# State products behind the preceding pair's outputs, and two of seven products in halves, in a scan kernel fused with a PReLU layer

## The chip, the cores and the metric

The kernel runs on one core of one Trainium2 chip. The metric is the device time of one execution in microseconds (us). The kernel before takes 374.15 us, the median of three runs (373.92 to 374.18). The profile is of one further execution of 374.39 us; its span, from the first instruction to the last, is 372.4 us.

## The reference

Two blocks follow one another. The first is a state-space scan over 4 batches, 8 heads and 768 tokens, in chunks; the second is a layer of width 2048 with a PReLU, on 3072 tokens of 256 numbers each. All is float32.

```python
# scan, per chunk (x: 4x8x768x32, a: 4x8x768, B and C: 4x8x768x16)
cum = np.cumsum(la, axis=-1)                       # la = log a of the chunk
L = np.exp(cum[..., :, None] - cum[..., None, :]) * causal
M = np.einsum('bhin,bhjn->bhij', Cc, Bc) * L       # gram products of C and B, decayed
y_intra = np.einsum('bhij,bhjd->bhid', M, xc)
y_inter = np.einsum('bhin,bhnd->bhid', Cc, state) * np.exp(cum)[..., None]
state = decay_full * state + sum_j(decay_from_j * B_j x_j)     # the state products
# layer (x: 3072x256, the scan's output with heads side by side)
h = x @ w_in                                       # 256 -> 2048
g = np.maximum(h, 0) + alpha * np.minimum(h, 0)
out = g @ w_out                                    # 2048 -> 256
```

(`state = ...` is cut to its meaning.) The kernel uses chunks of 128 tokens. Two chunks make a pair, and there are twelve pairs, 0 to 11; two pairs (512 tokens) make one of six groups.

## The kernel before

The first group goes through the layer with plain matrix products. Each later group goes through it as a two-by-two block product with seven products instead of eight, on each side. The 2048 hidden columns are taken in four quads (z = 0 to 3) per group; so there are 20 quads. A quad has seven products of the first part, from tokens to hidden values, which collect in two PSUM tiles A and Y. While they run, the seven products of the second part, from hidden values to outputs, run for the quad before. One product is two matrix instructions of 128x256 and appears as four records in the trace.

The order of a quad is fixed here. `after(j)` is a place at which other work is put in between:

```python
        first(A, lambda q: wi[:, q, 0, 0], b11, True)
        m1 = tile_of(wtp, "m1", "wt")
        nc.scalar.copy(out=m1, in_=A)
        after(1)
        first(Y, lambda q: s1[:, q], t1, True)
        m5 = tile_of(wtp, "m5", "wt")
        nc.scalar.copy(out=m5, in_=Y)
        after(2)
        after(3)
        first(A, lambda q: s2[:, q], t2)
        u2 = tile_of(wtp, "u2", "wg")
        nc.scalar.copy(out=u2, in_=A)
        after(4)
        nc.vector.tensor_tensor(out=Y, in0=Y, in1=u2, op=ALU.add)
        after(5)
        first(A, lambda q: wi[:, q, 1, 0], t3)
        c22 = tile_of(wtp, "c22", "wg")
        nc.vector.tensor_tensor(out=c22, in0=A, in1=m5, op=ALU.add)
        after(6)
        first(Y, lambda q: s4[:, q], b22)
        g12, g22, g21, g11 = (tile_of(gp, "gt", "gt") for i in range(4))
        prelu(g12, Y, z, 0)
        prelu(g22, c22, z, 1, (nc.scalar,))
        nc.scalar.copy(out=Y, in_=m1)
        prelu(g22, c22, z, 1, (nc.vector,))
        after(7)
        after(8)
        ta, tb, tc_, td = (tile_of(gp, "gt", "gt") for i in range(4))
        nc.gpsimd.tensor_tensor(out=tc_, in0=g22, in1=g12, op=ALU.subtract)
        first(A, lambda q: wi[:, q, 1, 1], t4)
        prelu(g21, A, z, 1)
        after(9)
        after(10)
        first(Y, lambda q: wi[:, q, 0, 1], b21)
        prelu(g11, Y, z, 0)
        for o, x0, x1 in ((ta, g12, g11), (tb, g22, ta), (td, tb, g21)):
            eng = nc.vector if g == NG - 1 and z == NZ - 1 and o is not td else nc.gpsimd
            eng.tensor_tensor(out=o, in0=x0, in1=x1, op=ALU.subtract)
        blocks[g, z] = {1: g11, 2: g21, 3: g22, 4: td, 5: ta, 6: tb, 7: tc_}
        after(11)
        after(12)
        after(13)
        after(14)
```

The products of the second part:

```python
    def product(g, z, n):

        if z == 0 and n == 1:
            ms[g] = [t.rearrange("p (h t) -> p h t", h=2)
                     for t in [bank(i) for i in range(3)] + m5_bank]
        i, h = (LAST if g == NG - 1 else HALVES)[n]
        s1, s2, s4 = out_sums
        for p in range(2):
            q = 2 * z + p
            w = {1: wq[:, q, 0, 0], 2: wq[:, q, 1, 0], 3: s4[:, q], 4: wq[:, q, 1, 1],
                 5: s1[:, q], 6: s2[:, q], 7: wq[:, q, 0, 1]}[n]
            nc.tensor.matmul(ms[g][i][:, h], w, blocks[g, z][n][:, p],
                             start=(q == 0 and h == 0), stop=(q == NQ - 1),
                             skip_group_check=True)
```

The scan of a pair of the next group is a generator of nine stages, put one by one into the places of the quads. Stage by stage for the pairs 4 to 11 (`fine`): transposes of B and C; four pieces of the decay matrix by scans on VectorE; state products and states; gram products of C and B and their multiplication by the decays in two stages; outputs and their copies. The state products are here, with `states`, which updates the state on VectorE and masks it on GpSimd:

```python
        def added(dps):
            dps = dps.rearrange("p (k m) -> p k m", m=P)
            for k in range(nk):
                for w in range(KC):
                    ws = slice(64 * w, 64 * w + 64)
                    nc.tensor.matmul(dps[ws, k], bn[:, k, ws], xt[:, k, w * P : (w + 1) * P],
                                     start=True, stop=True, tile_position=(0, 64 * w),
                                     skip_group_check=True)
            return dps
        # ... cut: states(dps)
        if fine:
            for k in range(2):
                for w in range(2):
                    half_decays(k, w)
                    if k == 1 and w == 1:
                        spread_c()
                    yield
        # ... cut: other pairs, gram products
            if fine:
                states(added(ss_tile()))
                c_decayed()
            yield
            gram = products_bc()
        # ... cut: multiplication of the gram products with the decays
        yield
        y = [ss_tile()[:, : 2 * Q].rearrange("p (k t) -> p k t", k=2) for w in range(KC)]
        # ... cut
        for k in range(2):
            if st[k] is not None:
                for w in range(KC):
                    ws = slice(64 * w, 64 * w + 64)
                    nc.tensor.matmul(y[w][:, k], st[k][ws], cd[ws, k], start=not begun, stop=False,
                                     tile_position=(64 * w, 0), skip_group_check=True)
                begun = True
        # ... cut: the outputs of the chunk itself, 32x128 products in columns of 32
        for w in range(KC):
            nc.scalar.copy(out=xts[g][:, w, q * Q : (q + 2) * Q],
                           in_=y[w].rearrange("p k t -> p (k t)"))
```

Two of the four gram tiles are in the small PSUM pool, the other two take the place of A and Y. Which stage falls into which place, and where the products of the second part go, say these tables (z, j) and j. A quad with gram products (z even, while scans are left) uses `with_gram`, the others `without`:

```python
    steps = {(0, 1): 0, (0, 2): 0, (0, 5): 0, (0, 9): 0, (0, 13): 0, (1, 1): 0, (1, 5): 0,
             (1, 12): 1, (1, 14): 1, (2, 1): 1, (2, 2): 1, (2, 5): 1, (2, 9): 1, (2, 13): 1,
             (3, 1): 1, (3, 5): 1, (3, 12): 2, (3, 14): 2}
# ... cut
    with_gram = {3: 1, 5: 2, 7: 3, 8: 5, 11: 7, 13: 6, 14: 4}
    without = {3: 1, 5: 2, 7: 3, 8: 5, 9: 7, 13: 6, 14: 4}
# ... cut, in after(j):
            places = with_gram if nxt < NP and z % 2 == 0 else without
            if i and j in places:
                product(*divmod(NZ + i - 1, NZ), places[j])
# ... cut
            if nxt + steps.get((z, j), NP) < NP:
                ssm(nxt + steps[z, j])
```

Of the kernel before, what the change touches and what calls it, by code (L numbers as in the profile page):

```python
# [9 lines left out]
F32 = mybir.dt.float32  # L10
U32 = mybir.dt.uint32
U16 = mybir.dt.uint16
ALU = mybir.AluOpType
# [9 lines left out]
def kernel(  # L23
# [25 lines left out]
    nc = tc.nc  # L49
# [276 lines left out]
    held = {}  # L326
    bns = {}

    def identity_bank():
# [82 lines left out]
    def spare():  # L412

        return ps_h.tile([P, GT], F32, name="hp", tag="hp")

    def pair(gp):

        b, c = divmod(2 * gp, CPB)
        nat, abc, xt, ap = loads["p", gp]
        last = c + 2 == CPB  # L420
        dec = work.tile([P, 2, H, Q], F32, name="dec")
        dv = dec.rearrange("p k h t -> p k (h t)")

# [37 lines left out]
            yield  # L461


        tp = spare() if gp == 1 else ss_tile()
        if gp == 0:
            keep_warm(tp, 3, Q)
# [23 lines left out]
        fine = gp >= 2 * GC // 2  # L490
        if gp < 2:
            spread_c()
        if gp == 0:
# [2 lines left out]
            dps = spare()  # L496
            keep_warm(dps, 6, Q)
            yield
        bn = bns.pop(gp) if gp in bns else pair_loads(gp)
        if gp == 1:  # L500
            c_decayed()
            dps = spare()
# [1 line left out]
        elif gp:  # L504
            yield

        nk = 1 if last else 2  # L510
        st = [masked.get(b)]
        new = work.tile([P, 2, P], F32, name="state")
        sm = work.tile([P, 2, P], F32, name="sm")

        def added(dps):
            dps = dps.rearrange("p (k m) -> p k m", m=P)
            for k in range(nk):
                for w in range(KC):
                    ws = slice(64 * w, 64 * w + 64)
                    nc.tensor.matmul(dps[ws, k], bn[:, k, ws], xt[:, k, w * P : (w + 1) * P],  # L520
                                     start=True, stop=True, tile_position=(0, 64 * w),
                                     skip_group_check=True)
            return dps

        def states(dps):
            for k in range(nk):
                old = state.get(b)
                if old is None:
                    nc.scalar.copy(out=new[:, k], in_=dps[:, k])
                else:  # L530
                    e = (k + 1) * Q - 1
                    nc.vector.scalar_tensor_tensor(out=new[:, k], in0=old, scalar=pf[:, e : e + 1],
                                                   in1=dps[:, k], op0=ALU.mult, op1=ALU.add)
                state[b] = new[:, k]
            nc.gpsimd.tensor_tensor(out=sm[:, :nk], in0=new[:, :nk],
                                    in1=hmask.unsqueeze(1).to_broadcast([P, nk, P]), op=ALU.mult)
            st.extend(sm[:, k] for k in range(nk))
            masked[b] = st[-1]

        if fine:  # L540
            for k in range(2):
                for w in range(2):
                    half_decays(k, w)
                    if k == 1 and w == 1:
                        spread_c()
                    yield
        else:
            if gp > 1:
                states(added(ss_tile()))
                c_decayed()  # L550
# [33 lines left out]
        if gp == 0:  # L584
            gram = products_bc()
            dps = added(dps)
            yield
            c_decayed()
            times(dec[:, :, :2], one_less(gram))
        elif gp == 1:  # L590
            gram = products_bc()
            g0 = one_less(gram)
            yield
            decays(1)
            states(dps)
            times(dec[:, :, :2], g0)
        else:
            if fine:
                states(added(ss_tile()))
                c_decayed()  # L600
            yield
            gram = products_bc()
        for i, r in enumerate(r for r in ((2, 3, 0, 1) if fine else (3, 2, 1, 0) if gp > 1 else range(4))
                              if r in gram):
# [6 lines left out]
        yield  # L611


        y = [ss_tile()[:, : 2 * Q].rearrange("p (k t) -> p k t", k=2) for w in range(KC)]
        if gp < 2:
            keep_warm(y[0].rearrange("p k t -> p (k t)"), 2 - gp)
        begun = False
# [7 lines left out]
        for k in range(2):  # L625
            for w in range(KC):
                for q in range(4):
                    h = 4 * w + q
                    nc.tensor.matmul(y[w][32 * q : 32 * q + 32, k], xt[:, k, h * D : (h + 1) * D],  # L629
                                     dec[:, k, h], start=False, stop=True,  # L630
                                     tile_position=(0, 32 * q), skip_group_check=True)
        g, q = divmod(2 * gp, GC)
        if q == 0:
            xts[g] = xtp.tile([P, KC, GT], F32, name="xT")
# [98 lines left out]
    LAST = {**HALVES, 4: (3, 1)}  # L733
    blocks = {}

    def product(g, z, n):

        if z == 0 and n == 1:
            ms[g] = [t.rearrange("p (h t) -> p h t", h=2)
                     for t in [bank(i) for i in range(3)] + m5_bank]  # L740
        i, h = (LAST if g == NG - 1 else HALVES)[n]
        s1, s2, s4 = out_sums
        for p in range(2):
            q = 2 * z + p
            w = {1: wq[:, q, 0, 0], 2: wq[:, q, 1, 0], 3: s4[:, q], 4: wq[:, q, 1, 1],
                 5: s1[:, q], 6: s2[:, q], 7: wq[:, q, 0, 1]}[n]
# [231 lines left out]
    for f in range(FIRST, NF):  # L978
        if f in (5, 10):
            load_pair(3 + f // 10)  # L980
        if f == 5:
            load_rows(1)
        hidden(0, f)
        if f <= 10:
            ssm(2)
        if f >= 9:
            ssm(3)
        for i in {FIRST: (5,), FIRST + 1: (6, 7)}.get(f, ()):
            convert_a(*pieces[i])
        convert_next(first=f > FIRST)  # L990
        if f == 8:
            bns[3] = pair_loads(3)
        if f == 8:
            rows_clamp(1)
            held["pr"] = rows_scan(1)
            rows_out(1)
        output(f - FIRST)
        if f in in_steps:
            weight_sums(wi, in_sums, 0, in_steps[f])
    early[0] = None  # L1000
    token_sums(1)
    ssm(2 * GC // 2, 2)


    steps = {(0, 1): 0, (0, 2): 0, (0, 5): 0, (0, 9): 0, (0, 13): 0, (1, 1): 0, (1, 5): 0,
             (1, 12): 1, (1, 14): 1, (2, 1): 1, (2, 2): 1, (2, 5): 1, (2, 9): 1, (2, 13): 1,
             (3, 1): 1, (3, 5): 1, (3, 12): 2, (3, 14): 2}

    late_sums = {(0, 2): ((wqt, out_sums, 0, 0),), (0, 4): ((wqt, out_sums, 0, 1),),
# [6 lines left out]
    last_out = {3: ((0, 0),), 5: ((1, 0),), 7: ((2, 0),), 8: ((3, 0),), 11: ((0, 1),), 13: ((1, 1),),  # L1016
            14: ((2, 1), (3, 1))}

    with_gram = {3: 1, 5: 2, 7: 3, 8: 5, 11: 7, 13: 6, 14: 4}
    without = {3: 1, 5: 2, 7: 3, 8: 5, 9: 7, 13: 6, 14: 4}  # L1020
    for i in range(NZ * (NG - 1)):
        g, z = divmod(NZ + i, NZ)
        nxt = 2 * g + 2

        def after(j, g=g, z=z, i=i, nxt=nxt):
            places = with_gram if nxt < NP and z % 2 == 0 else without
            if i and j in places:
                product(*divmod(NZ + i - 1, NZ), places[j])
            if i == 0:
                for f, half in last_out.get(j, ()):  # L1030
                    output(NF - LATE + f, half)
            if (i, j) in ((0, 13), (1, 2)):
                store_first(i)
            for args in late_sums.get((i, j), ()):
                weight_sums(*args)
            if g > 1 and z == 0 and j in (5, 9, 13, 14):
                if j == 5:
                    comb[0] = combine(g - 1)
                next(comb[0], None)
            if g > 1 and z in (1, 3) and j == 11:  # L1040
                finish(g - 1, z // 2)
            if nxt + steps.get((z, j), NP) < NP:
                ssm(nxt + steps[z, j])
            if nxt < NP and (z, j) == (3, 7):
                token_sums(g + 1)
            ahead = nxt + {(1, 3): 1, (3, 8): 2}.get((z, j), NP)
            if ahead < NP:
                if ahead == 6:
                    rows_turn(1, held["pr"])
                bns[ahead] = pair_loads(ahead)  # L1050

# [37 lines left out]
```

## Time and profile before

| engine | busy us | share of the span | instructions |
|---|---|---|---|
| TensorE, products | 365.4 | 98% | 2223 |
| TensorE, weight loads | 295.1 | 79% | 2223 |
| VectorE | 243.1 | 65% | 462 |
| GpSimd | 201.1 | 54% | 211 |
| ScalarE | 179.7 | 48% | 384 |

The products of the first part (line 772 of the kernel before, into `hp`, which is A and Y) are 33.7% of the chain that ended last, those of the second part (line 747, into `bank`) 32.4%. State products are line 520, transposes 469, gram products 570, outputs 622 and 629, the prelu 755 on ScalarE and 757 on VectorE, the copy that refills Y with m1 line 801. A line of the timeline begins with the start and the length in us. In brackets stands how long the engine was idle and what ended it. Products overlap in the engine's pipeline, so the lengths are not their cost; the distance from start to start is.

### The profile page before, as it was taken

The page shows a single profiled execution, that of the slowest core. Times are in us where ns is not written, and L with a number is a line of the kernel's source. Part 1 is how long each engine was busy: PE and PEld are TensorE (multiplying, and loading weights), DVE is VectorE, ACT ScalarE, POOL GpSimd, SP SyncE. Part 2 cuts the span into 40 slices and gives each one's busy share as a digit, 9 for nine tenths or more (in the row PEclk, how much of TensorE's full clock was granted, in tenths as well). Part 3 has the DMA queues.
Part 4 walks back from the last instruction along what each step waited for, and adds up shares of the span by engine and source line. Part 5 has one row for each costly group of instructions (what it writes and reads, how often), then busy time and mean ns, then how long its engine had stood idle before and what let it go on. Part 6 is the DMA issues. An engine that isn't in the chain of part 4 may idle for free.

```text
span 372.4 us, 6183 instructions
## 1 busy us (share of the span) xinstructions
PE 365.4 (98%) x2223; PEld 295.1 (79%) x2223; DVE 243.1 (65%) x462; ACT 179.7 (48%) x384; POOL 201.1 (54%) x211
## 2 busy tenths in 40 slices
PE   8989999999999999999999999999999999999996
PEld 8766666578788888788788788788788788888884
DVE  7897979976448548738638847637848644643364
ACT  1647866435355355444444445445535525553541
POOL 4775565778929754724644525555445355264512
PEclk9999999999999999999999999999999999999999
DMA  7889999911176301005603703702801001001004
GB/s 147 181 151 322 276 284 202 181 31 58 48 136 112 72 3 56 2 0 79 134 3 61 151 2 54 159 0 45 167 2 29 2 0 23 8 0 30 1 0 85
DMA packets 121878, 30.71 MB, mean 82 GB/s; under 512 B 93736, under 2 KB 117752, under 8 KB 121848
## 3 DMA queue, kind: packets, MB, share of 16 engines
q1 hardware_dynamic: 116736, 29.74, 36.0%
q10 hardware_dynamic: 5112, 0.59, 1.1%
q8 instruction: 17, 0.28, 0.3%
q14 instruction: 13, 0.11, 0.1%
HBM read 26.98 MB, written 3.34 MB: 81 GB/s over the span
## 4 chain that ended last, share of the span: by engine, by line
PE 86%; DVE 10%; DMA 2%; issue 1%; ACT 1%; POOLq 0%; DVEq 0%; SPq 0%
PE hp L772 34%; PE bank L747 32%; PE bank L686 4%; DVE dec L438 3%; PE hp L648 2%; PE ss L629 2%; PE ss L570 2%; DMA rows<-in_a_dram 2%; DVE wr L239 1%; PE hp L270 1%; PE ss L622 1%; DVE dec L432 1%; PE hp L570 1%; DVE gt L652 1%; PE ss L520 1%; PE hp L663 1%
## 5 line engine op out<-in xcount | busy, mean ns | idle before, releaser
L815 POOL TENSOR_TENSOR gt<-gt 128x512 f32<-128x512 f32 x58 | 73.6, 1268 | 30.8 <-DVE gt L757 23.9
L757 DVE SCALAR_TENSOR_TENSOR gt<-hp,s_mul,gt 128x256 f32<-128x256 f32 x120 | 52.5, 479 | 46.9 <-ACT gt L755 45.9
L747 PE MATMUL bank<-gt,w_out 128*128 128x256 f32 x320 | 82.4, 382 | 0.0
L755 ACT ACTIVATE gt<-hp,s_alpha 128x256 f32<-128x256 f32 x120 | 50.3, 470 | 46.7 <-PE hp L772 32.5
L747 PEld LDWEIGHTS bank<-gt,w_out 128*128 128x128 f32 x320 | 60.1, 190 | 10.4 <-issue 2.3
L806 POOL TENSOR_TENSOR gt<-gt 128x512 f32<-128x512 f32 x20 | 25.4, 1270 | 78.8 <-DVE gt L757 78.8
L747 PE MATMUL bank<-gt,ws 128*128 128x256 f32 x240 | 58.3, 379 | 0.0
L747 PEld LDWEIGHTS bank<-gt,ws 128*128 128x128 f32 x240 | 45.1, 190 | 5.8
L438 DVE TENSOR_TENSOR_SCAN dec<-abc,bank 128x256 f32<-128x256 f32 x80 | 48.1, 660 | 0.0
L772 PE MATMUL hp<-xs,w_in 128*128 128x256 f32 x160 | 42.9, 390 | 0.0
L772 PE MATMUL hp<-xT,w_in 128*128 128x256 f32 x160 | 41.9, 384 | 0.0
L772 PE MATMUL hp<-xs,ws 128*128 128x256 f32 x160 | 41.1, 379 | 0.0
L791 DVE TENSOR_TENSOR hp<-hp,u 128x512 f32<-128x512 f32 x20 | 14.0, 700 | 39.8 <-ACT u L789 39.8
L780 ACT COPY m<-hp 128x512 f32<-128x512 f32 x20 | 11.7, 586 | 51.8 <-PE hp L772 51.8
L772 PEld LDWEIGHTS hp<-xs,w_in 128*128 128x128 f32 x160 | 28.7, 189 | 7.7 <-issue 3.0
L772 PEld LDWEIGHTS hp<-xs,ws 128*128 128x128 f32 x160 | 30.4, 190 | 4.1
L772 PEld LDWEIGHTS hp<-xT,w_in 128*128 128x128 f32 x160 | 29.7, 190 | 5.0 <-issue 1.4
L686 PE MATMUL bank<-w_out,gt 128*128 128x256 f32 x128 | 31.0, 384 | 0.0
L686 PEld LDWEIGHTS bank<-w_out,gt 128*128 128x128 f32 x128 | 23.7, 190 | 6.6 <-issue 3.7
L795 DVE TENSOR_TENSOR c<-hp,m 128x512 f32<-128x512 f32 x20 | 13.6, 681 | 19.3 <-PE hp L772 19.3
L648 PE MATMUL hp<-xT,w_in 128*128 128x512 f32 x48 | 22.8, 597 | 0.4 <-DVE gt L652 0.2
L789 ACT COPY u<-hp 128x512 f32<-128x512 f32 x20 | 11.7, 585 | 22.5 <-PE hp L772 22.5
(156 smaller groups left out, 555.4 us busy)
## 6 DMA issues: line engine op xcount, KB each, us to landing
abc<-z SPq DMA_DIRECT2D x20, 512.0 KB, 5.0
raw<-in_moe_w_in_dram SPq DMA_DIRECT2D x8, 512.0 KB, 5.0
raw<-in_moe_w_out_dram SPq DMA_DIRECT2D x8, 512.0 KB, 6.9
xt<-in_x_dram SPq DMA_DIRECT2D x24, 128.0 KB, 2.8
out_dram<-o_sb SPq DMA_DIRECT2D x32, 64.0 KB, 1.9
nat<-in_B_dram SPq DMA_DIRECT2D x22, 64.0 KB, 3.3
nat<-in_C_dram SPq DMA_DIRECT2D x22, 64.0 KB, 2.7
ap<-pf SPq DMA_DIRECT2D x11, 128.0 KB
```

Of the source, the lines that this page charges most:

```text
L438: nc.vector.tensor_tensor_scan(out=dv[:, k, hs], data0=abc[k][:, hs], data1=ident_p[0], initial=0.0, op0=ALU.mult, op1=ALU.add)
L648: nc.tensor.matmul(hp, w_in[:, k, f * P : (f + 1) * P], xts[g][:, k], start=(k == 0), stop=(k == KC - 1))
L686: nc.tensor.matmul(pos[0][t // 2][:, t % 2], gt[:, t * Q : (t + 1) * Q], w_out[:, f], start=(f == 0 and t % 2 == 0), stop=(f == NF - 1), s ...
L747: nc.tensor.matmul(ms[g][i][:, h], w, blocks[g, z][n][:, p], start=(q == 0 and h == 0), stop=(q == NQ - 1), skip_group_check=True)
L755: nc.scalar.mul(o[:, p], h[:, p], s_alpha[:, fs[p]])
L757: nc.vector.scalar_tensor_tensor(out=o[:, p], in0=h[:, p], scalar=s_mul[:, fs[p]], in1=o[:, p], op0=ALU.mult, op1=ALU.max)
L772: nc.tensor.matmul(to[:, p], w(2 * z + p), b, start=start and p == 0, stop=True, skip_group_check=True)
L780: nc.scalar.copy(out=m1, in_=A)
L791: nc.vector.tensor_tensor(out=Y, in0=Y, in1=u2, op=ALU.add)
L795: nc.vector.tensor_tensor(out=c22, in0=A, in1=m5, op=ALU.add)
L806: nc.gpsimd.tensor_tensor(out=tc_, in0=g22, in1=g12, op=ALU.subtract)
L815: eng.tensor_tensor(out=o, in0=x0, in1=x1, op=ALU.subtract)
```

## The change

It moves the state products of the pairs 5 to 11 from the gram quad to the place right behind the outputs of the preceding pair, ahead of the copies of those outputs; they are written into the free half of the PSUM bank that holds one of the outputs. They are thus next to other products in tiles of part of the array, and the gram quad holds one small group less. That is meant to spare TensorE some of its changes between whole-array products and products in tiles. The stages of a pair become eleven, in another order: state products, states, transposes, decays, gram products, outputs, copies. Pair 4 has its state products before its transposes, ahead of the first quad. For the state products to come earlier, the decayed B (`bn`, on GpSimd) is formed earlier too, and the decayed C directly with the last decay.

In quads with gram products the products of the second part get other places: none is left between the second and the third product of the first part, and the products 2 and 5 are done in halves, one half in each of two places. That order is meant to give each copy and prelu products to run beside. The sums over a finished group (`combine`) follow to the places where their products are ready.

The diff, cut. The block from the transposes to `c_decayed` moves unchanged below `states` and is left out:

```diff
+        if fine:
+            bn = bns.pop(gp) if gp in bns else pair_loads(gp)
+            dps = added(beside.pop(gp) if gp in beside else ss_tile()[:, : 2 * Q])
+            yield
+            states(dps)
+            yield
...
                     if k == 1 and w == 1:
                         spread_c()
+                        c_decayed()
                     yield
...
-            if fine:
-                states(added(ss_tile()))
-                c_decayed()
-            yield
+            if not fine:
+                yield
             gram = products_bc()
...
-        y = [ss_tile()[:, : 2 * Q].rearrange("p (k t) -> p k t", k=2) for w in range(KC)]
+        ys = [ss_tile() for w in range(KC)]
+        y = [t[:, : 2 * Q].rearrange("p (k t) -> p k t", k=2) for t in ys]
+        if fine:
+            beside[gp + 1] = ys[1][:, 2 * Q :]
...
+        if fine:
+            yield
         g, q = divmod(2 * gp, GC)
...
-    def product(g, z, n):
-
-        if z == 0 and n == 1:
+    def product(g, z, n, parts=(0, 1)):
+
+        if g not in ms:
             ms[g] = [t.rearrange("p (h t) -> p h t", h=2)
                      for t in [bank(i) for i in range(3)] + m5_bank]
         i, h = (LAST if g == NG - 1 else HALVES)[n]
         s1, s2, s4 = out_sums
-        for p in range(2):
+        for p in parts:
...
+        if f == 14:
+            bns[4] = pair_loads(4)
...
-    ssm(2 * GC // 2, 2)
-
-
-    steps = {(0, 1): 0, (0, 2): 0, (0, 5): 0, (0, 9): 0, (0, 13): 0, (1, 1): 0, (1, 5): 0,
-             (1, 12): 1, (1, 14): 1, (2, 1): 1, (2, 2): 1, (2, 5): 1, (2, 9): 1, (2, 13): 1,
+    ssm(2 * GC // 2, 4)
+
+
+    steps = {(0, 1): 0, (0, 2): 0, (0, 5): 0, (0, 13): 0, (1, 1): 0, (1, 5): 0,
+             (1, 12): 1, (1, 14): 1, (2, 1): 1, (2, 2): 1, (2, 5): 1, (2, 13): 1,
              (3, 1): 1, (3, 5): 1, (3, 12): 2, (3, 14): 2}
...
-    with_gram = {3: 1, 5: 2, 7: 3, 8: 5, 11: 7, 13: 6, 14: 4}
-    without = {3: 1, 5: 2, 7: 3, 8: 5, 9: 7, 13: 6, 14: 4}
+    with_gram = {5: ((1,), (2, (0,))), 7: ((2, (1,)), (3,)), 8: ((5, (0,)),), 11: ((5, (1,)), (7,)),
+                 13: ((6,),), 14: ((4,),)}
+    without = {3: ((1,),), 5: ((2,),), 7: ((3,),), 8: ((5,),), 9: ((7,),), 13: ((6,),), 14: ((4,),)}
...
-            if i and j in places:
-                product(*divmod(NZ + i - 1, NZ), places[j])
+            for n in places.get(j, ()) if i else ():
+                product(*divmod(NZ + i - 1, NZ), *n)
...
-            if g > 1 and z == 0 and j in (5, 9, 13, 14):
-                if j == 5:
+            if g > 1 and z == 0 and j in (7, 11, 13, 14):
+                if j == 7:
...
                 ssm(nxt + steps[z, j])
+
+                if j == 5 and z % 2:
+                    for p in (1, 0, 1):
+                        if nxt + z // 2 + p < NP:
+                            ssm(nxt + z // 2 + p)
...
-            ahead = nxt + {(1, 3): 1, (3, 8): 2}.get((z, j), NP)
+            ahead = nxt + {(0, 9): 1, (2, 9): 2}.get((z, j), NP)
```

So a gram quad has, in TensorE's order (P for the second part, a and b for halves, names of the first part by what they read):

- before: A w11; Y s1; P1; A s2; P2; A w21; Y s4; P3; P5; A w22; state products; Y w12; P7; P6; gram; P4
- after: A w11; Y s1; A s2; P1; P2a; A w21; Y s4; P2b; P3; P5a; A w22; Y w12; P5b; P7; P6; gram; P4

The odd quads keep their order, with outputs behind P2, and after the change state products behind the outputs.

More of the change, by code (lines that the diff above doesn't have):

```diff
@@ L327 @@
     bns = {}
+    beside = {}
     def identity_bank():
@@ L420, in pair @@
         last = c + 2 == CPB
+        fine = gp >= 2 * GC // 2
         dec = work.tile([P, 2, H, Q], F32, name="dec")
@@ L461, in pair, with added, states @@
             yield
+        nk = 1 if last else 2
+        st = [masked.get(b)]
+        new = work.tile([P, 2, P], F32, name="state")
+        sm = work.tile([P, 2, P], F32, name="sm")
+        def added(dps):
+            dps = dps[:, : 2 * Q].rearrange("p (k m) -> p k m", m=P)
+            for k in range(nk):
+                for w in range(KC):
+                    ws = slice(64 * w, 64 * w + 64)
+                    nc.tensor.matmul(dps[ws, k], bn[:, k, ws], xt[:, k, w * P : (w + 1) * P],
+                                     start=True, stop=True, tile_position=(0, 64 * w),
+                                     skip_group_check=True)
+            return dps
+        def states(dps):
+            for k in range(nk):
+                old = state.get(b)
+                if old is None:
+                    nc.scalar.copy(out=new[:, k], in_=dps[:, k])
+                else:
+                    e = (k + 1) * Q - 1
+                    nc.vector.scalar_tensor_tensor(out=new[:, k], in0=old, scalar=pf[:, e : e + 1],
+                                                   in1=dps[:, k], op0=ALU.mult, op1=ALU.add)
+                state[b] = new[:, k]
+            nc.gpsimd.tensor_tensor(out=sm[:, :nk], in0=new[:, :nk],
+                                    in1=hmask.unsqueeze(1).to_broadcast([P, nk, P]), op=ALU.mult)
+            st.extend(sm[:, k] for k in range(nk))
+            masked[b] = st[-1]
+        if fine:
[4 more added lines that the diff above has]
+            yield
         tp = spare() if gp == 1 else ss_tile()
@@ L488, in c_decayed @@
                                     op=ALU.mult)
-        fine = gp >= 2 * GC // 2
         if gp < 2:
@@ L498, in pair @@
             yield
-        bn = bns.pop(gp) if gp in bns else pair_loads(gp)
+        if not fine:
+            bn = bns.pop(gp) if gp in bns else pair_loads(gp)
         if gp == 1:
@@ L505, in pair @@
             yield
[L510 to L538, printed above, removed]
         if fine:
@@ L597, in pair @@
         else:
-            if fine:
-                states(added(ss_tile()))
-                c_decayed()
-            yield
+            if not fine:
+                yield
             gram = products_bc()
```

## The prediction

> **What bounds the kernel now.** I read the engine shares of the page first, then the chain that ended last, then what TensorE waited for, and last the timeline of one quad with gram products. Shares and chain:
>
> ```profile
> span 372.4 us, 6183 instructions
> ...
> PE 365.4 (98%) x2223; PEld 295.1 (79%) x2223; DVE 243.1 (65%) x462; ACT 179.7 (48%) x384; POOL 201.1 (54%) x211
> ...
> PE 86%; DVE 10%; DMA 2%; issue 1%; ACT 1%; POOLq 0%; DVEq 0%; SPq 0%
> ```
>
> TensorE holds 86% of the chain, and from 98 us on (the quads) nearly all of it, so time is won there only by taking work, reloads or waits off TensorE. Of the list of waits two lines matter; each is us in total, times, longest:
>
> ```profile
> PEld hp L772 <- ACT u L789: 1.3, 6, 0.2
> ...
> PEld hp L570 <- DVE gt L757: 0.3, 1, 0.3
> ```
>
> The first is the third product into A waiting for ScalarE's copy of A (u2); the second is a gram product waiting for the last prelu. [...] So I read start against start in TensorE's timeline of the gram quad that begins at 112.32 us and of the odd quad after it:
>
> ```profile
> 116.70 1.10 PE L772 MATMUL hp<-xs,w_in 128*128 128x256 f32 x4
> 117.64 1.03 PE L772 MATMUL hp<-xT,ws 128*128 128x256 f32 x4
> 118.50 1.89 PE L747 MATMUL bank<-gt,ws 128*128 128x256 f32 x8
> 120.23 1.03 PE L772 MATMUL hp<-xs,w_in 128*128 128x256 f32 x4
> 121.19 0.44 PE L520 MATMUL ss<-xt,bn 128*64 128x128 f32 x4
> 121.56 1.13 PE L772 MATMUL hp<-xT,w_in 128*128 128x256 f32 x4
> 122.52 1.03 PE L747 MATMUL bank<-gt,w_out 128*128 128x256 f32 x4
> 123.39 1.03 PE L747 MATMUL bank<-gt,ws 128*128 128x256 f32 x4
> 124.34 0.48 PE L570 MATMUL ss<-cz,bc 32*128 32x256 f32 x2
> ...
> 125.64 1.13 PE L747 MATMUL bank<-gt,w_out 128*128 128x256 f32 x4
> ...
> 131.02 0.72 PE L622 MATMUL ss<-cd,sm 64*128 64x128 f32 x8
> 131.66 1.08 PE L629 MATMUL ss<-dec,xt 128*32 128x128 f32 x32
> ```
>
> The same timeline for all engines shows two operations that hold TensorE or nearly do (start, length, engine, line):
>
> ```profile
> 120.54 0.59 ACT L801 COPY hp<-m 128x512 f32<-128x512 f32 x1 [0.20 <-DVE gt L757]
> ...
> 123.66 0.87 DVE L757 SCALAR_TENSOR_TENSOR gt<-hp,s_mul,gt 128x256 f32<-128x256 f32 x2 [0.23 <-ACT gt L755]
> ```
>
> A product is four records here and takes 0.863 us from start to start when nothing holds it (118.50 to 120.23 is two of them), half a product 0.432. Anything beyond that is a loss, and there are four kinds:
> - The state products (121.19). The product before begins at 120.23 and should end at 121.09; the one after begins at 121.56 and its own successor at 122.52, 0.96 later. So they cost 122.52 − 0.86 − 121.09 = 0.57 us. This pair has one chunk (four records); pairs with two have eight, and by the same reading at 149 us cost 0.79. Four records are thus 0.22, and a fixed 0.35 is not arithmetic: 0.09 to enter the column tiling, 0.16 to leave it, 0.10 for the first product after it.
> - The gram products: 124.34 to 125.64 is 1.30 us. The earlier pair at 66.36 us took 1.07 to its successor. The fourth gram bank is Y's, which waits for the prelu from 123.66 to 124.53: 0.23 us lost. All seven later gram quads show 1.30.
> - u2: 116.70 to 117.64 is 0.94 instead of 0.86, and the start is 0.07 late: 0.14 us (0.08 in other quads).
> - The copy that refills Y with m1 (120.54) ends 3.49 us after the start of Y's product (117.64); in the later quads with this wait 3.54 to 3.59. At present the next product into Y starts 3.92 after it, so nothing is lost.
>
> **What the Trainium skill says.** "TensorEngine Tiling (Array Packing)", Key Properties, says that changing the tiling mode, not just the tile, drains the engine. The trace agrees: between the outputs in 64-row tiles (131.02) and those in 32-column tiles (131.66) lie 0.64 us for eight records worth 0.45 (a pair with four takes 0.42, so four are 0.22), and the 32 records in 32-column tiles take 1.01 us to the next product, of which 0.86 is arithmetic at 27 ns each: leaving that mode costs 0.15. State products use 64-column tiles, so behind the outputs they still change mode once more. "TensorE: Matmul & The Clock Gate", Step-by-step, says that weights of the next matmul are loaded while the present one runs; the trace agrees, loads lead by 0.2 us in full tiles and by nothing at a change of mode, whence the 0.10 after it. "PSUM — Partial Sum Buffer", PSUM bank collisions, says that two engines must not be in one bank and quadrant together, even at other columns. So with the state sums in the second half of an output's bank, the copies of the outputs and the state updates must follow one another; no run here shows a collision, but in the order of the changed kernel the first state update of such a pair does wait for ScalarE.
>
> **The change, part by part.** Seven pairs (5 to 11) get their state products behind the preceding pair's outputs; pair 4 gets them alone, ahead of its transposes, at unchanged cost.
>
> 1. State products moved. At the new place the outputs' exit (0.15) is paid before them, their own exit (0.16) after, and the slow first product once, as already now. They cost 0.22 or 0.43 of arithmetic plus 0.16 in place of plus 0.35. Saved: 0.20 × 7 = 1.4 us. No arithmetic goes.
>
> 2. Gram quads, the last stretch. Half of product 5 comes behind the last product into Y, so before the gram products stand 0.86 + 0.43 + 0.86 + 0.86 = 3.02 us instead of 2.59 plus the slow start. The prelu ended 2.97 us after Y's start (121.56 to 124.53), and the state update that stood before it on VectorE is gone. The 0.23 wait should vanish: 0.23 × 7 = 1.6 us saved.
>
> 3. Gram quads, the first stretch. Product 1 leaves its place between the second product (into Y) and the third (into A); products 1 and half of 2 stand after the third. u2 is then covered by 1.29 us. But the copy m1 now has only Y's product, 0.86 us, to hide in, and it ends 1.65 us after A's start, just as u2 did. One wait of 0.08 to 0.14 is exchanged for its twin: 0.
>
> 4. Gram quads, the middle. Between Y's product with s4 and Y's last product there are now half of 2, 3, half of 5 and A's product: with Y's own, 0.86 + 0.43 + 0.86 + 0.43 + 0.86 = 3.45 us. The state products, which stood there too, are gone. The copy into Y ends 3.49 to 3.59 after the start; a weight load begins about 0.05 us after its release and the product is effective 0.10 later (both read off u2: released at 116.56, it made the product 0.14 late where the load began 0.11 after it, 0.08 where 0.05). 3.54 + 0.15 − 3.45 = 0.24; for 3.59 it is 0.29, for 3.49 it is 0.19. Over the seven quads: 0.19 + 3 × 0.24 + 3 × 0.29 = 1.8 us, less 0.09 where the transpose of the decay rows falls in between: 1.7 us lost. The first quad (82 us), where outputs of the first part stand in place of products, has the same gap: another 0.2. Its gram wait (0.55) stays, as VectorE still has the weight sum ahead of the prelu.
>
> 5. VectorE's state updates, ScalarE's copies and GpSimd's masks move by half a quad. The update falls before c22 on VectorE, but A's next product comes 3.5 us after the product that c22 reads: hidden. GpSimd forms the decayed B earlier; loads of pair 8 are issued by 176 us, and the sum is due near 180: hidden, by a small margin.
>
> Sum: −1.4 − 1.6 + 0 + 1.7 + 0.2 = −1.1 us, so about 373.1.
>
> **Rivals.** (a) The middle wait does not appear, because ScalarE and VectorE reach Y's prelu sooner: the kernel gains 1.4 + 1.6 = 3 us, 371.1. For it: the change was evidently laid out around the gram wait, and halves are a tool of tuning. Against: the chain of product, ScalarE's prelu (118.70 to 119.54), VectorE's (119.58 to 120.46) and copy takes 3.49 or more in all twenty quads. (b) Tile modes of equal row count switch cheaply, so state products cost nearly their arithmetic: 0.16 × 7 more, 372.0. For it: both use all 128 rows; against: the skill's sentence, and the 64-row case. (c) New waits outweigh the gain: the masked states or the token sums, queued behind a later state update on GpSimd, or the m1 wait larger than u2's because ScalarE still has the transposes' copy; each 0.2 us in seven quads would be 1.4 us, 374.5. For it: GpSimd is in order and idles for others; against: token sums are used 7 us later, and before the copy of m1 ScalarE stood idle 1.66 us.
>
> **Range and chances.** The parts are each of 1.4 to 1.7 us with opposite signs, and each is uncertain by about half. Combined that is some 1 us either side: 371.5 to 374.5. Two per cent would be 7.5 us, and even if all three losses of a gram quad fell away, it would be (0.35 + 0.23 + 0.14) × 7 = 5.0 us. Within 2%: 0.985.
>
> **What would show it.** State products: behind the outputs, 0.37 or 0.59 to the next product. Gram: 1.07 us instead of 1.30. The third product into A: 0.08 to 0.14 late, u2's line gone from those quads, one for m1 in its place. Y's last product: some 0.25 late, and a line of TensorE waiting for ScalarE's copy hp (L801's counterpart) of about seven times 0.2. The prediction is wrong if that line is missing, if the gram stays at 1.30, or if waits on GpSimd appear on TensorE.

## The result

The changed kernel takes 373.39 us, the median of four runs (372.29 to 373.66), against 374.03 for the kernel before (373.25 to 374.18). The ratio is 0.9981 with a 95% interval of 0.9956 to 1.0006. So the gain of 0.6 us is smaller than the uncertainty of the comparison, which doesn't exclude that the times are equal. The prediction was 373.1, with 371.5 to 374.5 as its range, and that range holds the time before as well. What a change of this size is made of can only be read in the profile.

Engine shares and chain of the page of the changed kernel:

```profile
span 371.6 us, 6171 instructions
...
PE 363.5 (98%) x2223; PEld 291.6 (78%) x2223; DVE 246.2 (66%) x462; ACT 180.1 (48%) x384; POOL 201.5 (54%) x211
...
PE 83%; DVE 9%; DMA 3%; ACT 2%; issue 1%; ACTq 1%; POOLq 0%; SPq 0%; DVEq 0%
```

TensorE still carries the kernel, with as many records as before, 2223. ScalarE's share of the chain has gone from 1% to 2%. Of the two lines shown of before in the list of waits (total, times, longest), that for u2 has gone from 1.3 us in six waits to 0.6 in three, all in the last group, which has no gram products; one for m1, of 0.6 in three, has come. That for the gram products has grown from 0.3 to 0.6, still a single wait, in the first gram quad. A new line is the one that the prediction named as a sign:

```profile
PEld hp L785 <- ACT hp L814: 2.9, 8, 0.4
```

That is the weight load of Y's last product, waiting for the copy of m1 into Y. The 2.9 us are idle time of the weight load; the products are late by 1.8 us in all. What is lost stands in TensorE's timeline from start to start, here an odd quad, then a gram quad:

```profile
131.78 1.08 PE L640 MATMUL ss<-dec,xt 128*32 128x128 f32 x32
132.79 0.66 PE L478 MATMUL ss<-xt,bn 128*64 128x128 f32 x8
133.38 1.13 PE L785 MATMUL hp<-xs,w_in 128*128 128x256 f32 x4
...
171.10 1.97 PE L785 MATMUL hp<-xs,ws 128*128 128x256 f32 x8
172.91 1.46 PE L760 MATMUL bank<-gt,w_out 128*128 128x256 f32 x6
...
177.66 1.03 PE L785 MATMUL hp<-xs,w_in 128*128 128x256 f32 x4
...
179.63 0.59 PE L760 MATMUL bank<-gt,ws 128*128 128x256 f32 x2
...
181.88 0.48 PE L580 MATMUL ss<-cz,bc 32*128 32x256 f32 x2
...
182.96 1.13 PE L760 MATMUL bank<-gt,w_out 128*128 128x256 f32 x4
```

- 132.79 to 133.38: eight records of state products cost 0.59 us behind the outputs; at their old place such a visit (one group of state products between other work) cost 0.79.
- 171.10 to 172.91: Y's s1 and A's s2 product take 1.81 us instead of 1.73; 0.08 is the wait for m1, which replaces that for u2.
- 177.66 to 179.63: A's and Y's last products take 1.97 us instead of 1.73. That is the new wait, 0.24 us.
- The gram products of this quad, from 181.88 to 182.96, take 1.08 us instead of 1.30.

The span of a profile varies from run to run ahead of the quads: in the four runs that leave the state products in the gram quad the first quad begins between 81.35 and 82.64 us. So in what follows D stands for TensorE's distance from the start of the last product record of the first group before the quads (near 81 us) to the start of TensorE's last record of all (the expectations call it the last product). It holds all quads, and its parts repeat to a few hundredths where nothing is changed, but for the first gram quad (0.3 us in one run). D is 287.39 us before and 286.69 in the changed kernel: 0.70 less. Counted from the first quad, as three expectations below do, the distance is 0.65 shorter than D where pair 4 has its state products in its gram quad, and 1.39 shorter where they stand ahead of the first quad.

Each D is of one profile. Each ratio is to runs of the kernel before that were taken beside it, with medians of 373.95 to 374.09.

| kernel | D us | time, median us | ratio to before, 95% interval |
|---|---|---|---|
| before | 287.39 | 374.03 | |
| changed | 286.69 | 373.39 | 0.9981 (0.9956 to 1.0006) |
| e1, state products moved, old order | 288.22 | 375.05 | 1.0029 (1.0018 to 1.0040) |
| e2, old place, new order | 285.86 | 372.78 | 0.9967 (0.9956 to 0.9977) |
| e3, product 2 whole | 286.52 | 373.32 | 0.9986 (0.9978 to 0.9993) |
| e4, weight sum later | 286.05 | 372.86 | 0.9970 (0.9959 to 0.9982) |
| e5, old place, third order | 285.53 | 371.72 | 0.9945 (0.9932 to 0.9959) |
| e6, product 5 whole | 286.49 | 373.13 | 0.9972 (0.9964 to 0.9981) |
| e7, as e5, weight sum later | 285.20 | 371.96 | 0.9951 (0.9939 to 0.9964) |
| e8, state products twice | 289.24 | 375.72 | 1.0050 (1.0037 to 1.0062) |
| e9, as e3, transposition earlier | 285.74 | 372.34 | 0.9955 (0.9943 to 0.9968) |
| e10, as e9, weight sum later | 285.10 | 371.60 | 0.9931 (0.9918 to 0.9944) |

The theory to be tested: the move itself saves 0.20 us in each of seven pairs, but it takes away the cover under which the copy into Y was made; what the order wins at the gram products goes into that copy's wait. The rival: the gain is all from fewer changes of tiling mode, and the order is neutral.

### The profile page after: what moved, and what is told of

It is laid out like the page before. It is cut to its first block, busy times and chain, and to the rows that moved or that the text cites. A ratio compares the mean times of both kernels' runs of the same rounds, so it can differ in the third digit from the quotient of the medians.

```text
span 371.6 us, 6171 instructions
## 1 busy us (share of the span) xinstructions
PE 363.5 (98%) x2223; PEld 291.6 (78%) x2223; DVE 246.2 (66%) x462; ACT 180.1 (48%) x384; POOL 201.5 (54%) x211
## 4 chain that ended last, share of the span: by engine, by line
PE 83%; DVE 9%; DMA 3%; ACT 2%; issue 1%; ACTq 1%; POOLq 0%; SPq 0%; DVEq 0%
PE hp L785 34%; PE bank L760 32%; PE bank L699 3%; PE hp L661 2%; PE ss L640 2%; PE ss L580 2%; DVE dec L441 2%; DMA rows<-in_a_dram 2%; PE ss L633 1%; DVE wr L239 1%; DMA nat<-in_B_dram 1%; DVE dec L435 1%; PE ss L478 1%; PE hp L676 1%; PE ss L511 1%
## 5 line engine op out<-in xcount | busy, mean ns | idle before, releaser
L760 PE MATMUL bank<-gt,ws 128*128 128x256 f32 x240 | 59.5, 379 | 0.0
L493 POOL TENSOR_TENSOR sm<-state,bmask 128x256 f32<-128x256 f32 (+1 forms) x12 | 8.0, 663 | 34.8 <-DVE state L490 34.6
L770 DVE SCALAR_TENSOR_TENSOR gt<-c,s_mul,gt 128x256 f32<-128x256 f32 x40 | 20.8, 560 | 0.0
```

The costliest lines, as they stand in the source:

```text
L493: nc.gpsimd.tensor_tensor(out=sm[:, :nk], in0=new[:, :nk], in1=hmask.unsqueeze(1).to_broadcast([P, nk, P]), op=ALU.mult)
L760: nc.tensor.matmul(ms[g][i][:, h], w, blocks[g, z][n][:, p], start=(q == 0 and h == 0), stop=(q == NQ - 1), skip_group_check=True)
L770: nc.vector.scalar_tensor_tensor(out=o[:, p], in0=h[:, p], scalar=s_mul[:, fs[p]], in1=o[:, p], op0=ALU.mult, op1=ALU.max)
```

## Experiments

### The two parts one by one: e1 and e2

e1 is the changed kernel with the old order of products:

```diff
-    with_gram = {5: ((1,), (2, (0,))), 7: ((2, (1,)), (3,)), 8: ((5, (0,)),), 11: ((5, (1,)), (7,)),
-                 13: ((6,),), 14: ((4,),)}
+    with_gram = {3: ((1,),), 5: ((2,),), 7: ((3,),), 8: ((5,),), 11: ((7,),), 13: ((6,),), 14: ((4,),)}
...
-            if g > 1 and z == 0 and j in (7, 11, 13, 14):
-                if j == 7:
+            if g > 1 and z == 0 and j in (5, 9, 13, 14):
+                if j == 5:
```

> The changed kernel with the old order of the second part's products in gram quads; only the state products are moved. My theory: the move saves 0.20 us in each of seven pairs, but the products left between Y's product with s4 and Y's last one are as many as in the changed kernel, so the wait for the copy into Y (0.24 to 0.30 us, six quads) stays, and with only products 7 and 6 ahead of the gram products their wait of 0.15 to 0.23 us comes back: span about 1.0 to 1.6 us above the changed kernel's 371.6, that is 372.6 to 373.2, no better than before. Rival: all that the change gains comes from the fewer changes of tiling mode and the order is neutral; then the span is about 371.6 and the copy's wait is gone.

Measured: D is 288.22, 1.53 above the changed kernel and 0.83 above before; the time is 0.3% above before, and the interval excludes equality. Gram products take 1.30 us again, and the line of the wait for the copy reads as in the changed kernel, 2.9, 8, 0.4.

So the move alone makes the kernel slower: 1.4 us are saved on state products and about 1.8 lost on Y. Of the remaining 0.4 of the 0.83, 0.33 is in the first gram quad, of which e4 tells. The rival falls.

e2 is the kernel before with the new order; the state products stay in the gram quad:

```diff
-    with_gram = {3: 1, 5: 2, 7: 3, 8: 5, 11: 7, 13: 6, 14: 4}
+    with_gram = {5: ((1,), (2, (0,))), 7: ((2, (1,)), (3,)), 8: ((5, (0,)),), 11: ((5, (1,)), (7,)),
+                 13: ((6,),), 14: ((4,),)}
...
-            if g > 1 and z == 0 and j in (5, 9, 13, 14):
-                if j == 5:
+            if g > 1 and z == 0 and j in (7, 11, 13, 14):
+                if j == 7:
```

> The kernel before with the new order and the halves; the state products stay in the gram quad. My theory: the state products (0.57 or 0.79 us) then lie ahead of Y's last product and cover the copy's wait; the gram products take 1.07 us instead of 1.30; one wait of A is exchanged for the other. So 0.23 x 7 = 1.5 us are gained over before: span 370.8 to 371.0, about 0.7 us below the changed kernel. Rival: the order is neutral, span about 372.4 as before.

Measured: D is 285.86, which is 1.53 below before, as expected, and 0.83 below the changed kernel. The span of 371.4 is above the one expected because the part ahead of the quads began later in this profile; D does not contain it. Its gram products take 1.08 us in the seven quads, and ahead of Y's last product (178.77) nothing but the ordinary cost of state products is seen:

```profile
177.23 1.03 PE L772 MATMUL hp<-xs,w_in 128*128 128x256 f32 x4
178.18 0.66 PE L520 MATMUL ss<-xt,bn 128*64 128x128 f32 x8
178.77 1.13 PE L772 MATMUL hp<-xT,w_in 128*128 128x256 f32 x4
...
181.99 0.48 PE L570 MATMUL ss<-cz,bc 32*128 32x256 f32 x2
...
183.06 1.13 PE L747 MATMUL bank<-gt,w_out 128*128 128x256 f32 x4
```

The order of the products, with the state products at their old place, is thus worth twice the whole change. The two parts add up: +0.83 for the move and −1.53 for the order make the −0.70 of the changed kernel.

### Is it the copy into Y? e3, e6 and e9

e3 puts one more half of a product between Y's last two products, by taking it from ahead of A's product with t3:

```diff
-    with_gram = {5: ((1,), (2, (0,))), 7: ((2, (1,)), (3,)), 8: ((5, (0,)),), 11: ((5, (1,)), (7,)),
+    with_gram = {5: ((1,),), 7: ((2,), (3,)), 8: ((5, (0,)),), 11: ((5, (1,)), (7,)),
```

> The changed kernel with product 2 whole behind Y's product with s4, none of it ahead of A's product with t3. My theory: Y's two products are then 3.88 us apart, more than the 3.70 to 3.76 that the copy needs, so the waits of 0.24 to 0.30 us (1.6 us in all) vanish; A's product with t3 waits for u2 again, 0.08 to 0.14 us in seven quads (0.8 us). Span about 370.8. Rival: the wait before Y's last product is not for the copy but for the prelu of A (c22) or for ScalarE's queue, which the later products push back too; then it stays and the span grows by 0.8 us to 372.4.

Measured: D is 286.52, only 0.17 below the changed kernel instead of 0.8. The wait of Y's last product is gone, and the wait for u2 is there, as expected; but Y's product with s4 is late too, by 0.20 us in three quads with z = 2 and by 0.08 in two with z = 0, 0.76 in all. VectorE's timeline of one with 0.20:

```profile
170.26 0.70 DVE L904 STREAM_TRANSPOSE o_sb<-c 128x512 f32<-128x512 f32 x1
170.89 3.54 DVE L441 TENSOR_TENSOR_SCAN dec<-abc,bank 128x256 f32<-128x256 f32 x6
174.35 0.67 DVE L804 TENSOR_TENSOR hp<-hp,u 128x512 f32<-128x512 f32 x1
```

The addition of u2 into Y (line 804), for which that product waits, begins without any idle time behind six scans, although u2 was there at 173.96 (ScalarE's copy from 173.37, 0.59 long). With product 1 no longer ahead of A's product with t2, u2 comes some 0.8 us earlier in the quad than in the kernel before, and VectorE isn't ready for it. Neither theory had this wait.

e6 reaches the same distance between Y's products in another way, from behind, and leaves the first half of the quad alone:

```diff
-    with_gram = {5: ((1,), (2, (0,))), 7: ((2, (1,)), (3,)), 8: ((5, (0,)),), 11: ((5, (1,)), (7,)),
+    with_gram = {5: ((1,), (2, (0,))), 7: ((2, (1,)), (3,)), 8: ((5,),), 11: ((7,),),
```

> The changed kernel with product 5 whole ahead of A's last product, so that only products 7 and 6 lie between Y's last product and the gram products. Nothing else is changed, so VectorE's scans stay where they were. My theory: the wait for the copy into Y (six quads, 1.6 us) vanishes and the wait of the gram products (0.15 to 0.23 us in seven quads, 1.0 to 1.6 us) comes back: from the first quad to the last product 284.7 to 285.3 us against 285.3. That is, halving product 5 only chooses between two waits of equal size. Rival: the halves were worth their own; then the wait for the copy stays beside the gram's and it is 286.5 or more.

Measured: D is 286.49; from the first quad 285.10. The wait for the copy has left the sixty longest, and the gram products take 1.30 us again in the seven quads. That is what was expected: half a product is moved from one wait to another of the same size.

e9 is e3 with VectorE's 0.70 us transposition of finished outputs (line 904), which runs just ahead of the six scans, three places earlier:

```diff
-            if g > 1 and z in (1, 3) and j == 11:
+            if g > 1 and z in (1, 3) and j == 8:
                 finish(g - 1, z // 2)
```

> The changed kernel with product 2 whole behind Y's product with s4, as in the run that gained only 0.17 us, and with VectorE's transposition of a finished group's outputs (0.70 us, in odd quads) three places earlier, into a gap of VectorE before the prelu of A. My theory: that run lost its gain because A's product with t2 and so u2 come 0.86 us earlier, and the addition of u2 into Y then stands behind six scans which start late because of the transposition (three quads, 0.20 us each). With the transposition out of the way the addition runs at once: 0.6 us less than that run, 285.9 us from the last product before the quads to the last product. Rival: the addition waits for ScalarE's copy and not for VectorE's queue; then it stays at 286.5.

Measured: D is 285.74, 0.78 below e3. The scans begin directly behind the prelu, and the addition now waits for ScalarE:

```profile
169.52 3.57 DVE L441 TENSOR_TENSOR_SCAN dec<-abc,bank 128x256 f32<-128x256 f32 x6
173.25 0.70 DVE L804 TENSOR_TENSOR hp<-hp,u 128x512 f32<-128x512 f32 x1 [0.16 <-ACT u L802]
```

So it was VectorE's queue that ate e3's gain; 0.78 us come back where 0.6 was expected, because the two smaller waits go too. Without it, the arrangement is 0.95 below the changed kernel; 0.8 had been the sum for e3.

### The first gram quad: e4

In the first gram quad (from 82.7 us) the gram products take 1.95 us in the changed kernel, more than the 1.62 of before. In VectorE's timeline of the changed kernel the sum of weights (line 728) stands ahead of the last prelu:

```profile
93.45 1.07 DVE L728 TENSOR_TENSOR w_out<-w_out 128x512 f32<-128x512 f32 x1
94.44 0.86 DVE L770 SCALAR_TENSOR_TENSOR gt<-hp,s_mul,gt 128x256 f32<-128x256 f32 x2
```

```diff
-                 (0, 10): ((wqt, out_sums, 0, 3, nc.vector),), (1, 2): ((wi, in_sums, 4, 1),),
+                 (0, 12): ((wqt, out_sums, 0, 3, nc.vector),), (1, 2): ((wi, in_sums, 4, 1),),
```

> The changed kernel with VectorE's weight sum of the first quad put behind the last prelu instead of ahead of it. My theory: the gram products of that quad take 1.95 us because the last prelu queues behind the sum (1.07 us on VectorE); with the sum later they take 1.1 to 1.2 us: span about 370.8. Rival: they wait for ScalarE or for the gram multiplication's buffers, and the span stays at 371.6.

Measured: D is 286.05, 0.64 below the changed kernel. The prelu comes first and ends 0.6 us earlier, counted from the first quad's start (82.45 there, 82.73 in the changed kernel), and the gram products take 1.30 us:

```profile
93.50 0.88 DVE L770 SCALAR_TENSOR_TENSOR gt<-hp,s_mul,gt 128x256 f32<-128x256 f32 x2 [0.25 <-ACT gt L768]
94.29 0.68 DVE L728 TENSOR_TENSOR w_out<-w_out 128x512 f32<-128x512 f32 x1
```

So the sum's place ahead of the prelu is shown to be the cause of the wait. That 1.30 us are left instead of 1.1 to 1.2 fits the seven other gram quads of e1 and e6, which have only two products ahead of the gram products too and take 1.30.

### Are the fixed costs per visit? e8

```diff
-            dps = added(beside.pop(gp) if gp in beside else ss_tile()[:, : 2 * Q])
+            room = beside.pop(gp) if gp in beside else ss_tile()[:, : 2 * Q]
+            added(room)
+            dps = added(room)
```

> The changed kernel with each group of state products computed twice in a row, into the same place. My theory: the fixed part of their cost is paid once per visit, for the changes of tiling mode, and not per product; so only arithmetic is added, 0.43 us for the five pairs with two chunks and 0.22 for the three with one: 2.8 us in all, the cost of a visit 1.02 and 0.59. Rival: the fixed part belongs to the products themselves (their semaphores, the first write into a bank); then another 0.16 us each is added, 4.1 us in all.

Measured: over the eight pairs the visits take 6.88 us, against 4.05 in the changed kernel; 2.83 more, where 2.8 was expected and 4.1 was the rival's. A visit with sixteen records ends after 1.03 us:

```profile
132.03 1.09 PE L478 MATMUL ss<-xt,bn 128*64 128x128 f32 x16
133.06 1.13 PE L787 MATMUL hp<-xs,w_in 128*128 128x256 f32 x4
```

The fixed 0.16 us is paid once per visit. D rose by only 2.55, since the gram products of the first quad happened to wait 0.29 less (1.66 us); the sum of weights ahead of their prelu took 0.77 us there.

### Leaving the state products where they were: e5, e7 and e10

e5 is e2 with half of product 1 ahead of A's product with t2, and product 2 whole:

```diff
-    with_gram = {3: 1, 5: 2, 7: 3, 8: 5, 11: 7, 13: 6, 14: 4}
+    with_gram = {3: ((1, (0,)),), 5: ((1, (1,)), (2,)), 7: ((3,),), 8: ((5, (0,)),),
+                 11: ((5, (1,)), (7,)), 13: ((6,),), 14: ((4,),)}
```

> The kernel before with the state products left in the gram quad and a third order of the second part: half of product 1 between Y's first and A's second product, the other half and product 2 behind it, products 3 and half of 5 behind Y's product with s4, then A, the state products, Y, half of 5, 7 and 6. My theory: every copy and prelu is covered (m1 by 1.29 us, u2 by 1.29, the gram products by 3.02); only where a pair has one chunk is Y's last product 0.1 to 0.2 us late. So the state products at their old place cost 1.4 us in all, but no wait is left: from the first quad to the last product 284.8 us, against 285.3 in the changed kernel and 286.7 before. Rival: as in the run with product 2 whole, the earlier product of A meets VectorE's scans and a new wait appears; then 285.3 or more.

Measured: from the first quad 284.88, D 285.53, 1.86 below before. In the quad at 140 us no product but the two at the changes of tiling mode takes more than its 0.863 us:

```profile
147.32 1.03 PE L772 MATMUL hp<-xs,w_in 128*128 128x256 f32 x4
148.28 0.66 PE L520 MATMUL ss<-xt,bn 128*64 128x128 f32 x8
148.87 1.13 PE L772 MATMUL hp<-xT,w_in 128*128 128x256 f32 x4
149.83 0.59 PE L747 MATMUL bank<-gt,ws 128*128 128x256 f32 x2
```

Where a pair has one chunk, Y's last product is 0.06, 0.16 and 0.11 us late, and in one quad the gram products take 1.23 us instead of 1.08. The rival's wait for VectorE does not appear: u2 comes only 0.43 us earlier here.

e7 is e5 with the later weight sum of e4:

> As the run with the state products left in the gram quad and half of product 1 first, and with VectorE's weight sum of the first quad behind the last prelu. My theory: the two savings add, as they lie in different quads: 0.3 to 0.5 us less in the first gram quad (1.62 to about 1.2), so from the first quad to the last product 284.4 us, 0.6 % under before in all. Rival: in the first quad the state updates, which stay ahead of the prelu in this order, hold the gram products by themselves; then no change.

Measured: D is 285.20, and the gram products of the first quad take 1.30 us instead of 1.62. In the timed runs the 0.3 us can't be told from nothing (371.96 against 371.72).

e10 is e9 with the later weight sum, so it keeps the state products behind the outputs:

> The same with VectorE's weight sum of the first quad behind the last prelu. My theory: another 0.6 us less, as in the changed kernel alone: 285.3 us from the last product before the quads to the last product, and about 371.7 us in all, equal to the best order with the state products left in the gram quad. Rival: the two do not add, because the sum then delays the scans that follow; 285.9.

Measured: D is 285.10, 0.64 below e9, and the time is 371.60 us, a ratio of 0.9931 to before. It is the fastest of all, with e5 and e7 within their uncertainty. But e10 and e7 reach nearly the same D with different losses. In e10 two waits stand open in each gram quad. In the one at 170 us Y's s1 and A's s2 product take 1.81 us instead of 1.73, which is the wait for m1, and A's next product, with t3, takes 0.94 to its successor instead of 0.86, which is the wait for u2. Over the seven quads they are 1.6 us. e7 has neither, but pays 1.4 us more for the visits. No run has the state products moved and all four waits (for m1, for u2, for the copy into Y, of the gram products) covered, so what the move is worth when it uncovers nothing is not shown.

## Why the prediction was right

The time lay 0.3 us above the predicted 373.1, well within the range. As the range held the time before too, it is the parts that bear the prediction out. Summed from TensorE's distances of the two profiles:

| step of the prediction | predicted us | measured us |
|---|---|---|
| 1, state products moved | −1.4 | −1.40: 0.37 and 0.59 a visit instead of 0.57 and 0.79 |
| 2, gram products | −1.6 | −1.53: six quads 1.30 to 1.08, one to 1.11 |
| 3, m1 for u2 | 0 | 0.00: 0.81 in both kernels |
| 4, copy into Y | +1.7 | +1.63: three quads of 0.30 and three of 0.24 |
| 4, first quad, copy into Y | +0.2 | +0.19 |
| 4, first quad, gram products | 0 | +0.33 |
| pair 4's state products; transpose of the decay rows in its new place | 0 | −0.04; +0.08 |
| sum | −1.1 | −0.74 |

D itself fell by 0.70; the remaining 0.04 is spread in thousandths over many quads. Step by step:

Step 1 held to the hundredth: behind the outputs a visit pays one change of mode, 0.16 us. That going from 32-column to 64-column tiles costs as much as leaving tiles altogether agrees with "TensorEngine Tiling (Array Packing)", Key Properties, in the Trainium skill, which has TensorE drained at each change of mode but gives no cost; e8 shows the cost to be one per visit. Rival (b), cheap switching among tiles of equal row count, is refuted: the outputs in 32-column tiles take 1.01 us to the next start, whether full tiles or state products follow.

Step 2 and step 4 held in size, and e1, e2 and e6 show each to be what it was said to be: half a product may lie under the copy or ahead of the gram products, and is missing at the other. In one detail step 4 was wrong: the transpose of the decay rows falls into the gram quad that begins at 112.99 us and leaves nothing of that quad's wait, where the prediction had taken 0.09 off its 0.19. So six quads lose, not seven; that the sum is near all the same, 1.63 against 1.7, is partly luck, as the six lose 0.04 more than forecast. Rival (a), no wait at the copy, is refuted by the list of waits.

Step 3 is the exchange of two equal waits. e5 shows that both can be saved by half of product 1 in the old place, and e3 and e9 that product order also moves the hour at which VectorE is needed; the prediction had looked for that only on VectorE's state updates.

The mis-sized term is in step 4's last sentence, that the gram wait of the first quad stays at 0.55. It became 0.88, as the sum of weights ahead of the prelu took 1.07 us on VectorE instead of 0.68. e4 shows the sum's place to be the cause of the wait, and in e8, with the sum at 0.77, the wait is 0.29 shorter. Why the sum took longer no run was made to separate, but the traces point one way. Two lines of the kernel before, then GpSimd's of the changed one, whose sum (93.45, 1.07) stands under e4:

```profile
93.53 0.68 DVE L715 TENSOR_TENSOR w_out<-w_out 128x512 f32<-128x512 f32 x1
93.75 1.04 POOL L535 TENSOR_TENSOR sm<-state,bmask 128x256 f32<-128x256 f32 x1 [1.24 <-DVE state L532]
...
93.33 0.64 POOL L387 TENSOR_TENSOR bn<-nat,prt 128x256 f32<-128x256 f32 x1
```

Before, the sum began first, and GpSimd's masking of the state, 0.22 us later, took 1.04 us; in e7, where the sum comes after it, the same masking takes 0.73. In the changed kernel GpSimd began the decayed B 0.12 us ahead of the sum, and it was the sum that took longer; in e7 the sum begins 0.16 us behind another operation of GpSimd and takes 1.11. In these pairs the one that began later was the longer; that this is the cause is argued, not tested.

Step 5 held: in the quads TensorE waits for GpSimd only once, 0.4 us in the first quad, as in the kernel before, and never for a transfer; rival (c) did not come about.

## What to carry to other kernels

When TensorE is never idle for long, ask of each small group of products not only what it costs but what it covers: a detour of 0.79 us that shelters a copy can be worth more than the 0.20 us that a better place for it saves. Add up, for each buffer that is refilled, the work between two uses against the chain that refills it, and share out the movable products by these sums; half a product is a useful unit. And check the other engines' queues at the new hour: an earlier result is worth nothing if the engine that takes it is in the middle of scans.

## What was not expected

The addition of u2 in e3 was held up by work of VectorE that had no connection with it, a 0.70 us transposition that began 4.1 us earlier; moving it was worth 0.78 us, more than the 0.70 of the whole change. And the same 128x512 sum on VectorE took 0.68 us in one kernel and 1.07 in another, where GpSimd had begun an operation just ahead of it.
